# Up projection once per row pair with the signs joined on VectorE, and the down projection with stationary weights, in a float32 Fourier-mixing MLP

## The chip, the cores and the metric

The kernel runs on one core of a Trainium2 chip. The metric is the device time of one execution in microseconds (us), the median of three runs. Engines go by their short names: PE is TensorE (PEld its weight loads), DVE is VectorE, ACT is ScalarE, POOL is GpSimd, SP is SyncE, which here only issues DMAs. An engine works through its own instructions in order; it waits for another engine or for a DMA through semaphores.

## The reference

```python
X = np.fft.fft(x, axis=1); X = np.fft.fft(X, axis=2)     # x: (8, 3008, 256) float32
x = X.real.astype(np.float32).reshape(24064, 256)
h = x @ w_in                                             # (256, 2048)
g = np.maximum(0.01 * h, h)
return (g @ w_out).astype(np.float32)                    # (2048, 256)
```

Sequence and features of eight batches are mixed by a Fourier transform of which the real part is kept; a two-layer perceptron with a leaky ReLU follows. The weights arrive as float64.

## The kernel before

All arithmetic is float32. One `nc.tensor.matmul` of float32 operands is two PE instructions, each with a weight load of its own, so every count of the trace is twice that of the code.

The real part is cosine times cosine minus sine times sine. The rows of a batch are folded (row s with row S-s) by `fold_x`, so that the sequence transform needs only a quarter of the lengths, and the feature transform is multiplied into `w_in` once, on the chip (`w_in_part`), into the table `wf`. What is left per batch is `dft`: for a unit, that is a batch b and a half c of 377 or 376 frequencies, four products of six matmuls each give the even and odd parts of the cosine half (`mix0`) and of the sine half (`mix1`), and `butterfly` adds and subtracts them. A unit has a plus part and a minus part (`sg`), and each of these stands for two output rows that differ only in the sign of the sine half: a row pair.

A tile (list `tiles`) is one of these rows sets, 375 to 377 tokens; there are 4 in a unit, 64 in all. For each tile `up` goes over the 16 blocks of 128 hidden features: two matmuls into one PSUM bank, the cosine half with `wf[:, 0]` and the sine half with one of the two signed copies `wf[:, 1]` and `wf[:, 2]`; then ACT makes 0.01 times the bank (line 314) and DVE the maximum (line 315). `down` takes 128 tokens at a time as the stationary operand, streams the 256 columns of `w_out` past them, sums 16 blocks in one bank, and ACT copies it out (line 326) to be stored by SP, tokens in rows.

PSUM has eight banks: three for `up`, three for `dft`, two for `down`. The frequency d = 128 has no sine; it is computed for all batches in the start (`nyquist`) and a small DMA puts it into row 0 of `mix1`.

Two buffers, `xa` and `xb`, hold x of one batch: `xa` the rows, `xb` their mirrors, gathered by indirect DMAs that POOL issues. The folded rows end in `xb`. The next batch's rows may land when `dft` of the second half has read `xb` for the last time. In the start, eight pieces of `w_in` and then eight of `w_out` are loaded by SP and rounded from float64 to float32 by seven DVE instructions each (lines 214 to 220), through six buffers `g`.

A scheduler orders the instructions of each engine by its own estimate of time, so an engine's order differs from the order in the code.

Of the kernel before, what the change touches and what calls it, by code (L numbers as in the profile page):

```python
# [80 lines left out]
def feat_tables():  # L81
    """[j, (cosines 0..127 | cosine 128, -sines | cosine 128, +sines)], by shape alone."""
# [5 lines left out]
    out = np.zeros((D, 3, P), np.float32)  # L88
    out[:, 0] = cos
    for w, sign in ((1, -1.0), (2, 1.0)):  # L90
        out[:, w] = sign * sin
        out[:, w, 0:1] = nyq
    return out.reshape(D, 3 * P)
# [3 lines left out]
def tile_fnet_leaky_relu(  # L97
# [14 lines left out]
    work = ctx.enter_context(tc.tile_pool(name="work", bufs=1))  # L112
    ps = ctx.enter_context(tc.tile_pool(name="ps", bufs=1, space=PS))

    def up_ps():
        return ps.tile([P, 512], F32, tag="up", bufs=3, name="up_ps")

    def dft_ps():
        return ps.tile([P, 512], F32, tag="dft", bufs=3, name="dft_ps")
# [261 lines left out]
```

## Time and profile before

| | |
|---|---|
| time, median of 3 runs | 2948.84 us (2948.0 to 2951.03) |
| span of the profiled execution | 2950.5 us |
| PE busy | 2910.1 us, 99% |
| DVE busy | 707.3 us, 24% |
| ACT busy | 593.5 us, 20% |
| `down` on PE (line 323) | 45% of the chain that ended last |
| `up` on PE (line 311) | 44% |
| `dft` on PE (line 252) | 9% |

The chain that ended last is followed back from the last instruction, at each step to what released it. Here nearly all of it is PE, one instruction after another. The mean time of a matmul (479 ns) is longer than its distance from the next one, since matmuls are pipelined; distances are taken from runs of many matmuls in the chain.

### The profile page before, as it was taken

Reading aid. Unit: us, or ns where it says so; the run is one execution under the profiler, and the core shown is the slowest. Engines: PE = TensorE matmul, PEld = TensorE weight load, DVE = VectorE, ACT = ScalarE, POOL = GpSimd, SP = SyncE. Lnnn points to the kernel's source line nnn. Section 1 sums busy time; section 2 is a strip of 40 time slices with the busy share of each in tenths; the row PEclk is TensorE's granted clock in tenths of the full one; section 3 lists DMA queues with packets and bytes.
Section 4 is the critical chain, followed back from the end, with each engine's and each line's share of the span. In section 5 each row is a group of like instructions: output and inputs, shape, how many; then the busy total and the mean of one; then the engine's idle time right before and its main releaser. Section 6 shows DMA issues by size and latency. Waiting matters only on the chain.

```text
span 2950.5 us, 26768 instructions
## 1 busy us (share of the span) xinstructions
PE 2910.1 (99%) x11104; PEld 2090.8 (71%) x11104; DVE 707.3 (24%) x1270; ACT 593.5 (20%) x1279; POOL 79.1 (3%) x115
## 2 busy tenths in 40 slices
PE   4999999999999999999999999999999999999999
PEld 1667777777777677677677777777777776776777
DVE  6431221321222211221212212222212212112111
ACT  1121121221221211221221212212212112112211
POOL 2010000100001000000000000010000000000000
PEclk8999999999999999999999999999999999999999
DMA  8010000100001000010000000010000100000000
GB/s 295 18 50 11 7 9 11 50 9 9 9 9 51 7 11 11 9 50 9 7 11 27 32 11 7 9 51 9 9 11 6 32 11 6 11 10 7 11 11 11
DMA packets 40736, 69.24 MB, mean 23 GB/s; under 512 B 5942, under 2 KB 30374, under 8 KB 39590
## 3 DMA queue, kind: packets, MB, share of 16 engines
q1 hardware_dynamic: 31334, 33.53, 3.5%
q0 software_dynamic: 8128, 24.73, 2.7%
q10 hardware_dynamic: 1152, 9.27, 0.8%
q8 instruction: 87, 1.43, 0.2%
q14 instruction: 35, 0.29, 0.0%
HBM read 42.82 MB, written 24.64 MB: 23 GB/s over the span
## 4 chain that ended last, share of the span: by engine, by line
PE 98%; DMA 1%; DVE 1%; issue 0%; SPq 0%; ACT 0%; DVEq 0%
PE down_ps L323 45%; PE up_ps L311 44%; PE dft_ps L252 9%; DMA g<-in_w_in_dram 1%; DMA nya<-in_x_nyq_dram 1%; PE up_ps L234 0%; DVE xa L162 0%; DVE g L219 0%; DVE g L215 0%; DVE xb L170 0%; DVE xb L169 0%; DVE g L216 0%; DVE g L218 0%; DVE g L217 0%; DVE win L220 0%; DVE g L214 0%
## 5 line engine op out<-in xcount | busy, mean ns | idle before, releaser
L323 PE MATMUL down_ps<-wo,g 128*128 128x256 f32 x6144 | 1336.5, 379 | 0.0
L311 PE MATMUL up_ps<-mix,wf 128*128 128x376 f32 (+2 forms) x4096 | 1309.2, 479 | 0.0
L323 PEld LDWEIGHTS down_ps<-wo,g 128*128 128x128 f32 x6144 | 1153.3, 188 | 185.1
L311 PEld LDWEIGHTS up_ps<-mix,wf 128*128 128x128 f32 x4096 | 776.6, 190 | 505.3 <-issue 0.6
L315 DVE TENSOR_TENSOR g<-up_ps,leak 128x376 f32<-128x376 f32 (+2 forms) x1024 | 562.9, 550 | 1955.1 <-ACT leak L314 1955.1
L314 ACT ACTIVATE leak<-up_ps 128x376 f32<-128x376 f32 (+2 forms) x1024 | 495.4, 484 | 923.9 <-PE up_ps L311 920.8
L326 ACT COPY o<-down_ps 128x256 f32<-128x256 f32 (+2 forms) x192 | 71.4, 372 | 1185.8 <-PE down_ps L323 1185.8
L252 PE MATMUL dft_ps<-tab,xb 128*128 128x377 f32 (+3 forms) x768 | 248.5, 479 | 0.0
L252 PEld LDWEIGHTS dft_ps<-tab,xb 128*128 128x128 f32 (+1 forms) x768 | 145.4, 189 | 98.3 <-issue 0.6
L234 PE MATMUL up_ps<-win,feat_sb 128*128 128x512 f32 x48 | 30.9, 798 | 37.1 <-DVE win L220 18.7
L258 DVE TENSOR_TENSOR mix<-ev,dft_ps 128x377 f32<-128x377 f32 (+1 forms) x32 | 17.5, 547 | 198.4 <-PE dft_ps L252 198.4
L135 POOL DMA_DIRECT2D xb<-in_x_dram x8 | 4.0, 500 | 2158.0 <-PE dft_ps L252 2028.8
L234 PEld LDWEIGHTS up_ps<-win,feat_sb 128*128 128x128 f32 x48 | 11.4, 252 | 55.7 <-issue 29.0
L140 POOL DMA_INDIRECT xb<-in_x_dram,mirror x48 | 46.6, 971 | 21.7 <-issue 13.4
L257 ACT COPY ev<-dft_ps 128x377 f32<-128x377 f32 (+3 forms) x34 | 16.1, 472 | 124.0 <-PE dft_ps L252 124.0
L162 DVE TENSOR_TENSOR xa<-xa,xb 128x2550 f32<-128x2550 f32 (+1 forms) x16 | 28.0, 1748 | 31.8 <-DMA xb<-in_x_dram,mirror 31.8
L259 DVE TENSOR_TENSOR mix<-ev,dft_ps 128x377 f32<-128x377 f32 (+1 forms) x32 | 17.3, 541 | 0.0
L252 PE MATMUL dft_ps<-tab,nya 128*8 128x377 f32 (+3 forms) x48 | 15.7, 479 | 0.0
L171 ACT COPY xb<-xa 128x10 f32<-128x10 f32 (+1 forms) x16 | 3.2, 202 | 61.7 <-POOL xb L172 56.7
L170 DVE TENSOR_TENSOR xb<-xa 128x1270 f32<-128x1270 f32 (+1 forms) x16 | 15.1, 946 | 0.0
L169 DVE TENSOR_TENSOR xb<-xa 128x1270 f32<-128x1270 f32 (+1 forms) x16 | 15.1, 946 | 0.0
L235 ACT COPY wf<-up_ps 128x512 f32<-128x512 f32 x12 | 6.9, 585 | 39.5 <-PE up_ps L234 39.5
(25 smaller groups left out, 99.3 us busy)
## 6 DMA issues: line engine op xcount, KB each, us to landing
out_dram<-o SPq DMA_DIRECT2D x128, 128.0 KB
xa<-in_x_dram POOLq DMA_DIRECT2D x8, 1280.0 KB
tab<-in_seq_tab_dram ACTq DMA_DIRECT2D x8, 1131.0 KB
g<-in_w_in_dram SPq DMA_DIRECT2D x8, 512.0 KB
g<-in_w_out_dram SPq DMA_DIRECT2D x8, 512.0 KB
out_dram<-o SPq DMA_DIRECT2D x32, 120.0 KB
out_dram<-o SPq DMA_DIRECT2D x16, 121.0 KB
out_dram<-o SPq DMA_DIRECT2D x16, 119.0 KB
```

What stands on the lines that cost most here:

```text
L140: nc.gpsimd.indirect_dma_start(out=bv[0:n, i, :], out_offset=None, in_=pairs, in_offset=bass.IndirectOffsetOnAxis(ap=mirror[0:n, b, i : i ...
L162: nc.vector.tensor_tensor(a[:, :, :, 1:D], a[:, :, :, 1:D], m[:, :, ::-1, D - 1 : 0 : -1], op=ALU.add)
L234: nc.tensor.matmul(pt, lhsT=feat_sb[:, a, w * P : (w + 1) * P], rhs=win[a], start=(a == 0), stop=(a == 1))
L252: nc.tensor.matmul(ps_t[0:m, 0 : KW[c]], lhsT=z_of(i), rhs=tabs[n, c][0 : NV[i], i, 0 : KW[c]], start=(i == 0), stop=(i == NI - 1))
L257: nc.scalar.copy(ev[0:m, 0:kw], even_ps[0:m, 0:kw])
L258: nc.vector.tensor_tensor(plus, ev[0:m, 0:kw], odd_ps[0:m, 0:kw], op=ALU.add)
L259: nc.vector.tensor_tensor(minus, ev[0:m, 0:kw], odd_ps[0:m, 0:kw], op=ALU.subtract)
L311: nc.tensor.matmul(pt[:, 0:n], lhsT=wf[:, 0 if blk == 0 else w, fs], rhs=t[:, ::-1] if back else t, start=(blk == 0), stop=(blk == 1))
L314: nc.scalar.activation(leak[:, 0:n], pt[:, 0:n], ACT.Copy, bias=0.0, scale=SLOPE)
L315: nc.vector.tensor_tensor(g[:, f, 0:n], pt[:, 0:n], leak[:, 0:n], op=ALU.max)
L323: nc.tensor.matmul(pt[0:nr, 0:D], lhsT=hidden[j, f // FQ][:, f % FQ, t0 : t0 + nr], rhs=wo[:, f, :], start=(f == 0), stop=(f == NF - 1))
L326: nc.scalar.copy(o[0:nr, :], pt[0:nr, 0:D])
```

## The change

`tiles` goes; a block `(b, c, sg)` is a row pair, 32 in all. For one of its 16 hidden blocks (a step) `up` does the cosine half and the sine half once, each into a bank of its own. DVE then adds the d = 128 term, spread over all partitions (`nb`, one number `wn` per hidden feature), to the cosine bank, and forms the sum and the difference with the sine bank; ACT applies its leaky ReLU to both at once, in place. `down` takes `w_out` as the stationary operand and the hidden tokens as the moving one: two halves of the 256 output columns by two rows of the pair, summed over 16 steps in four banks. The result is stored transposed, [column, token], and the host puts it in order. `down` of a step follows `up` by two steps. `up` and `dft` share four banks.

Beside that, x and its mirrors come laid out by the host, so that two plain DMAs on SP load a batch into one buffer `xt`; the third copy in `wf` goes; the numbers `wn` take 32 matmuls of one column; the buffers for weights are three instead of six.

```diff
-        return ps.tile([P, 512], F32, tag="up", bufs=3, name="up_ps")
+    def up_ps(name="up_ps"):
+        return ps.tile([P, 512], F32, tag="up", bufs=4, name=name)
 ...
+        t = xp.tile([P, 2, NI, 2, D], F32, tag="x", bufs=1, name="xt")
+        for h in range(2):
+            nc.sync.dma_start(t[:, h], x[b, h])
 ...
+        nc.vector.tensor_tensor(s, s, z, op=ALU.add)
+        lo, hi = s[:, :, 1:P], s[:, :, P + 1 : D]
+        nc.vector.tensor_tensor(z[:, :, 1:P], lo, hi, op=ALU.add)
+        nc.vector.tensor_tensor(z[:, :, P + 1 : D], lo, hi, op=ALU.subtract)
 ...
-        return work.tile([P, FQ, KC], F32, tag="g", bufs=6, name="g").rearrange("p f k -> p (f k)")
+        return work.tile([P, 4, KC], F32, tag="raw", bufs=3, name="raw").rearrange("p f k -> p (f k)")
 ...
-        for w in range(3):
+        for w in range(2):
 ...
+        for i in range(WN // P):
+            for a in range(2):
+                nc.tensor.matmul(pt[:, i : i + 1], lhsT=win[a][:, i * P : (i + 1) * P],
+                                 rhs=feat_sb[:, a, 2 * P : 2 * P + 1], start=(a == 0), stop=(a == 1))
+        nc.scalar.copy(wn[:, f0 // P : f0 // P + WN // P], pt[:, 0 : WN // P])
 ...
+    def spread(u):
+        b, c = u
+        t = work.tile([P, 2, KC], F32, tag="nb", bufs=2, name="nb")
+        nc.sync.dma_start(t[:, :, 0 : KW[c]], nyq_dram[b, c, :, 0 : KW[c]].partition_broadcast(P))
+        spreads[u] = t
 ...
+    def up(j, f):
+        b, c, sg, _, n = blocks[j]
+        fs = slice(f * P, (f + 1) * P)
+        pt = [up_ps("cos_ps"), up_ps("sin_ps")]
+        for blk in range(2):
+            nc.tensor.matmul(pt[blk][:, 0:n], lhsT=wf[:, blk, fs], rhs=mixed[b, c][blk][:, sg, 0:n], start=True, stop=True)
+        cos = work.tile([P, KC], F32, tag="cos", bufs=3, name="cos")
+        nc.vector.scalar_tensor_tensor(cos[:, 0:n], in0=spreads[b, c][:, sg, 0:n], scalar=wn[:, f : f + 1],
+                                       in1=pt[0][:, 0:n], op0=ALU.mult, op1=ALU.add)
+        g = work.tile([P, 2, KC], F32, tag="g", bufs=5, name="g")
+        nc.vector.tensor_tensor(g[:, 0, 0:n], cos[:, 0:n], pt[1][:, 0:n], op=ALU.add)
+        nc.vector.tensor_tensor(g[:, 1, 0:n], cos[:, 0:n], pt[1][:, 0:n], op=ALU.subtract)
+        nc.scalar.activation(g[:, :, 0:n], g[:, :, 0:n], ACT.Lrelu)
+        hidden[j, f] = g
+
+    def down(j, f):
+        _, _, _, first, n = blocks[j]
+        if f == 0:
+            sums[j] = [[ps.tile([P, 512], F32, tag="sum", bufs=4, name="sum_ps") for _ in range(2)] for _ in range(2)]
+        g = hidden.pop((j, f))
+        for h in range(2):
+            for i in range(2):
+                nc.tensor.matmul(sums[j][h][i][:, 0:n], lhsT=wo[:, f, h * P : (h + 1) * P], rhs=g[:, i, 0:n],
                                  start=(f == 0), stop=(f == NF - 1))
 ...
+    lag = 2
+    for at in range(len(steps) + lag):
+        if at < len(steps):
+            j, f = steps[at]
+            up(j, f)
 ...
+            if sg == 1 and f == 10 and c == 0 and b + 1 < B:
+                load_x(b + 1)
+            if n + 1 < len(units):
+                if sg == 0 and f == 8:
+                    spread(units[n + 1])
+                    if c == 1:
+                        fold_x(b + 1)
+                if sg == 1 and f in (2, 8):
+                    dft(units[n + 1], f // 8)
+        if at >= lag:
+            down(*steps[at - lag])
```

How the instructions of an engine stand, at three places. First PE, in the middle of a unit of the first batch, before: the end of `up` of one tile and the beginning of `down` of the tile ahead of it (`wf` and `wo` are the weights, `g` the hidden tokens; the number behind a name is the buffer's).

```order
L311 MATMUL up_ps_547<-mix0_276,wf_84 128x376 [waits DVE_49]
L311 MATMUL up_ps_547<-mix1_295,wf_84 128x376
L311 MATMUL up_ps_553<-mix0_276,wf_84 128x376 [waits DVE_49]
L311 MATMUL up_ps_553<-mix1_295,wf_84 128x376
L311 MATMUL up_ps_559<-mix0_276,wf_84 128x376 [waits DVE_49]
L311 MATMUL up_ps_559<-mix1_295,wf_84 128x376
L323 MATMUL down_ps_565<-wo_85,g_421 128x256 x4
L323 MATMUL down_ps_565<-wo_85,g_446 128x256 x4
```

After, one and a half steps in the middle of a block; `wf` meets the cosine half `mix0` and the sine half `mix1` in banks of their own, and `wo` meets one `g` in four banks.

```order
L312 MATMUL cos_ps_530<-mix0_274,wf_74 128x377 [waits DVE_49]
L312 MATMUL sin_ps_531<-mix1_293,wf_74 128x377 [waits DVE_49]
L329 MATMUL sum_ps_452<-g_508,wo_76 128x377 [waits Activation_49]
L329 MATMUL sum_ps_453<-g_508,wo_76 128x377
L329 MATMUL sum_ps_454<-g_508,wo_76 128x377
L329 MATMUL sum_ps_455<-g_508,wo_76 128x377
L312 MATMUL cos_ps_546<-mix0_274,wf_74 128x377 [waits DVE_49]
L312 MATMUL sin_ps_547<-mix1_293,wf_74 128x377 [waits DVE_49]
```

Each hidden block of `up` was one bank with two matmuls; it is two banks with one each, and `down`, which was 48 matmuls of 256 columns in one stretch with a group of 16 for each bank, now comes in groups of four of 377 columns that visit four banks. Where there were four tiles in a unit, there are two blocks.

Second DVE, where x of the second batch is folded, before: `mix` is the second half of the unit's sine part, made when `dft` has ended, and lines 162 to 170 are `fold_x`.

```order
L258 TENSOR_TENSOR mix_700<-ev,dft_ps 128x376 [waits PE_49,Activation_49]
L259 TENSOR_TENSOR mix_700<-ev,dft_ps 128x376
L315 TENSOR_TENSOR g<-up_ps,leak 128x377 [waits Activation_49] x4
L162 TENSOR_TENSOR xa<-xa,xb 128x10x255 [waits DMASW6_49,DMASW2_49,DMASW7_49,DMASW1_49,DMASW0_49]
L163 TENSOR_TENSOR xa<-xa,xb 128x10
L162 TENSOR_TENSOR xa<-xa,xb 113x2x255 [waits DMASW5_49,DMASW4_49,DMASW3_49]
L163 TENSOR_TENSOR xa<-xa,xb 113x2
L169 TENSOR_TENSOR xb<-xa 128x10x127 [waits DVE_49,Pool_49]
L170 TENSOR_TENSOR xb<-xa 128x10x127
```

After, the same place; `xt` is the buffer of x, line 314 the new step on the cosine bank, lines 317 and 318 the sum and the difference.

```order
L269 TENSOR_TENSOR mix1_797<-ev_812,dft_ps_799 128x376
L314 SCALAR_TENSOR_TENSOR cos_824<-nb_312,wn_75,cos_ps_820 128x377 [waits PE_49]
L317 TENSOR_TENSOR g_826<-cos_824,sin_ps_821 128x377 [waits DVE_49,PE_49]
L318 TENSOR_TENSOR g_826<-cos_824,sin_ps_821 128x377
L314 SCALAR_TENSOR_TENSOR cos_838<-nb_312,wn_75,cos_ps_834 128x377 [waits PE_49]
L317 TENSOR_TENSOR g_840<-cos_838,sin_ps_835 128x377 [waits DVE_49,PE_49]
L318 TENSOR_TENSOR g_840<-cos_838,sin_ps_835 128x377
L314 SCALAR_TENSOR_TENSOR cos_855<-nb_312,wn_75,cos_ps_851 128x377 [waits PE_49]
L170 TENSOR_TENSOR xt_844<-xt_844 128x3072 [waits DMAHW3_49,DMAHW2_49,Pool_49]
L317 TENSOR_TENSOR g_857<-cos_855,sin_ps_852 128x377 [waits DVE_49,PE_49]
L318 TENSOR_TENSOR g_857<-cos_855,sin_ps_852 128x377
L314 SCALAR_TENSOR_TENSOR cos_869<-nb_312,wn_75,cos_ps_865 128x377 [waits PE_49]
L172 TENSOR_TENSOR xt_844<-xt_844 128x12x127 [waits DVE_49]
```

The fold is three large instructions instead of eight, and it stands between the instructions of the third, fourth and fifth steps behind the butterfly, though the code calls it later; the first of them waits for both halves of the load.

Third SP, at the beginning of the program, before:

```order
L177 DMA feat_sb_69<-in_feat_tab_dram 128x2x384
L198 DMA g_108<-in_w_in_dram 128x1024
L132 DMA nya_86<-in_x_nyq_dram 128x5x16
L133 DMA nya_86<-in_x_nyq_dram 112x16
L134 DMA nya_86<-in_x_nyq_dram 1x16
L135 DMA nyb_87<-in_x_nyq_dram 1x8
L198 DMA g_119<-in_w_in_dram 128x1024 [waits DMAHW0_49]
L136 DMA nyb_87<-in_x_nyq_dram 1x8 [waits DMAHW1_49]
L198 DMA g_142<-in_w_in_dram 128x1024 [waits DMAHW3_49]
L198 DMA g_153<-in_w_in_dram 128x1024 [waits DMAHW5_49,DMAHW2_49,DVE_49]
```

After:

```order
L180 DMA feat_sb_69<-in_feat_tab_dram 128x2x258
L160 DMA xt_71<-in_x_dram 128x3072 x2
L202 DMA raw_91<-in_w_in_dram 128x1024
L257 DMA nyx_77<-in_x_nyq_dram 128x192 [waits DMAHW0_49]
L202 DMA raw_102<-in_w_in_dram 128x1024 [waits DMAHW2_49]
L202 DMA raw_131<-in_w_in_dram 128x1024 [waits DMAHW4_49,DVE_49]
L202 DMA raw_142<-in_w_in_dram 128x1024 [waits DMAHW6_49,DVE_49]
L202 DMA raw_171<-in_w_in_dram 128x1024 [waits DMAHW2_49,DMAHW0_49,DVE_49]
```

The two loads of x, 1.5 MB each, which were issued by POOL on its own queue, now stand ahead of the first piece of `w_in` on SP's, and the third piece already waits for DVE, where before it was the fourth.

## Rows read from the trace of the kernel before

**Rows 1.** The page's part 1: busy time, share of the span and instructions.
```profile
...
PE 2910.1 (99%) x11104; PEld 2090.8 (71%) x11104; DVE 707.3 (24%) x1270; ACT 593.5 (20%) x1279; POOL 79.1 (3%) x115
...
```

**Rows 2.** Stretches: length, busy us (instructions) of each engine, granted clock, DMA share, GB/s.
```profile
...
0.00:98.90 98.90, 61.84 (x145) 24.48 (x145) 64.04 (x128) 10.38 (x19) 18.32 (x27) 0.90 0.66 231
98.90:2947.20 2848.30, 2848.29 (x10961) 2066.30 (x10960) 643.22 (x1142) 582.75 (x1259) 60.80 (x88) 1.00 0.05 16
2947.20:2950.50 3.30, 0.00 (x0) 0.00 (x0) 0.00 (x0) 0.37 (x1) 0.00 (x0) 1.00 0.14 37
...
```

**Rows 3.** Groups by line: operation, shapes, count, busy us, mean ns, idle before.
```profile
...
L323 PE MATMUL down_ps<-wo,g 128*128 128x256 f32 x6144 | 1336.5, 379 | 0.0
L311 PE MATMUL up_ps<-mix,wf 128*128 128x376 f32 (+2 forms) x4096 | 1309.2, 479 | 0.0
...
L315 DVE TENSOR_TENSOR g<-up_ps,leak 128x376 f32<-128x376 f32 (+2 forms) x1024 | 562.9, 550 | 1955.1 <-ACT leak L314 1955.1
L314 ACT ACTIVATE leak<-up_ps 128x376 f32<-128x376 f32 (+2 forms) x1024 | 495.4, 484 | 923.9 <-PE up_ps L311 920.8 <-DVE g L315 3.1
...
L234 PEld LDWEIGHTS up_ps<-win,feat_sb 128*128 128x128 f32 x48 | 11.4, 252 | 55.7 <-issue 29.0 <-DVE g L219 18.4 <-DVE win L220 8.3
...
L235 ACT COPY wf<-up_ps 128x512 f32<-128x512 f32 x12 | 6.9, 585 | 39.5 <-PE up_ps L234 39.5
...
```

**Rows 4.** Chain that ended last, 55 to 200 us: start, length, what.
```profile
...
60.36 8.37 PE up_ps L234 x12
68.73 30.20 PE dft_ps L252 x94
...
132.04 20.72 PE down_ps L323 x96
152.76 15.16 PE up_ps L311 x48
167.93 7.59 PE dft_ps L252 x24
...
```

**Rows 5.** Timeline, weight loads and conversions: start, length, instruction, idle time before it.
```profile
...
1.26 0.45 SPq L198 DMA_DIRECT2D g<-in_w_in_dram  x1
...
6.84 0.36 SPq L198 DMA_DIRECT2D g<-in_w_in_dram  x1
...
14.70 0.43 DVE L214 TENSOR_SCALAR g<-g 128x512 int32<-128x512 int32 x1 [14.70 <-DMA g<-in_w_in_dram]
...
21.36 0.43 DVE L214 TENSOR_SCALAR g<-g 128x512 int32<-128x512 int32 x1 [3.05 <-DMA g<-in_w_in_dram]
...
...
60.13 0.42 DVE L214 TENSOR_SCALAR g<-g 128x512 int32<-128x512 int32 x1
60.47 0.68 DVE L220 SCALAR_TENSOR_TENSOR win<-g 128x512 f32<-128x512 f32 x1
...
63.66 0.42 DVE L214 TENSOR_SCALAR g<-g 128x512 int32<-128x512 int32 x1
...
```

**Rows 6.** Timeline, reload and fold of x around 176 to 194 us.
```profile
...
176.06 0.50 POOL L135 DMA_DIRECT2D xb<-in_x_dram  x1 [129.15 <-issue]
...
183.69 0.93 POOL L140 DMA_INDIRECT xb<-in_x_dram,mirror  x1 [0.30 <-issue]
186.28 2.81 DVE L162 TENSOR_TENSOR xa<-xa,xb 128x2550 f32<-128x2550 f32 x1 [4.59 <-DMA xb<-in_x_dram,mirror]
...
193.88 0.94 POOL L132 DMA_DIRECT2D xa<-in_x_dram  x1 [3.93 <-DVE xb L170]
...
```

**Rows 7.** Stretches, transfer of the direct half of x.
```profile
...
195.00:200.00 5.00, 5.00 (x25) 4.24 (x24) 0.00 (x0) 0.00 (x0) 0.89 (x2) 1.00 0.89 264
200.00:205.00 5.00, 5.00 (x20) 3.29 (x19) 1.09 (x2) 1.35 (x3) 0.00 (x0) 1.00 0.30 95
...
```

**Rows 8.** Stretch in the start in which PE works with gaps.
```profile
...
20.00:30.00 10.00, 7.11 (x11) 2.36 (x9) 4.38 (x10) 1.67 (x3) 6.02 (x6) 0.83 1.01 368
...
```

**Rows 9.** Timeline, ACT at the end of the span.
```profile
...
2947.23 0.37 ACT L326 COPY o<-down_ps 120x256 f32<-120x256 f32 x1 [6.53 <-PE down_ps L323]
```

More of the change, by code (lines that the diff above doesn't have):

```diff
@@ L87, in feat_tables, with chunks, columns @@
     nyq = np.where(j % 2 == 0, 1.0, -1.0)
[L88 to L93, printed above, removed]
+    out = np.zeros((D, 2 * P + 2), np.float32)
+    out[:, 0:P] = cos
+    out[:, P : 2 * P] = -sin
+    out[:, 2 * P :] = nyq
+    return out
+def chunks():
+    out, at = [], 0
+    for b in range(B):
+        for c in range(2):
+            for sg in range(2):
+                out.append((b, c, sg, at, KW[c]))
+                at += 2 * KW[c]
+    return out, at
+def columns():
+    at = np.zeros(B * S, np.int64)
+    for b, c, sg, first, n in chunks()[0]:
+        k = K0[c] + np.arange(n)
+        plus, minus = (k, (S - k) % S) if sg == 0 else ((H + k) % S, H - k)
+        at[b * S + minus] = first + n + np.arange(n)
+        at[b * S + plus] = first + np.arange(n)
+    return at
 @with_exitstack
@@ L300, in tile_fnet_leaky_relu @@
-    hidden = {}
-    def up(j, fq):
-        u, sg, w, k, n, _, back = tiles[j]
-        g = work.tile([P, FQ, KC], F32, tag="g", bufs=6, name="g")
-        hidden[j, fq] = g
-        for f in range(FQ):
-            pt = up_ps()
-            fs = slice((fq * FQ + f) * P, (fq * FQ + f + 1) * P)
-            for blk in range(2):
-                t = mixed[u][blk][:, sg, k : k + n]
-                nc.tensor.matmul(pt[:, 0:n], lhsT=wf[:, 0 if blk == 0 else w, fs],
-                                 rhs=t[:, ::-1] if back else t, start=(blk == 0), stop=(blk == 1))
-            leak = work.tile([P, KC], F32, tag="leak", bufs=3, name="leak")
-            nc.scalar.activation(leak[:, 0:n], pt[:, 0:n], ACT.Copy, bias=0.0, scale=SLOPE)
-            nc.vector.tensor_tensor(g[:, f, 0:n], pt[:, 0:n], leak[:, 0:n], op=ALU.max)
@@ L317, in down @@
-    def down(j):
-        _, _, _, _, n, first, _ = tiles[j]
-        for t0 in range(0, n, P):
-            nr = min(P, n - t0)
-            pt = down_ps()
-            for f in range(NF):
-                nc.tensor.matmul(pt[0:nr, 0:D], lhsT=hidden[j, f // FQ][:, f % FQ, t0 : t0 + nr], rhs=wo[:, f, :],
-                                 start=(f == 0), stop=(f == NF - 1))
-            o = work.tile([P, D], F32, tag="o", bufs=4, name="o")
-            nc.scalar.copy(o[0:nr, :], pt[0:nr, 0:D])
-            nc.sync.dma_start(out[first + t0 : first + t0 + nr, :], o[0:nr, :])
+            sequence(pt, B, lambda i: nya[:, i, r, :], r, c)
@@ new lines, in tile_fnet_leaky_relu @@
+    units = [(b, c) for b in range(B) for c in range(2)]
+    blocks, _ = chunks()
+    steps = [(j, f) for j in range(len(blocks)) for f in range(NF)]
+    def up(j, f):
[12 more added lines that the diff above has]
+        hidden[j, f] = g
@@ new lines, in down @@
+    def down(j, f):
[6 more added lines that the diff above has]
+                nc.tensor.matmul(sums[j][h][i][:, 0:n], lhsT=wo[:, f, h * P : (h + 1) * P], rhs=g[:, i, 0:n],
+                                 start=(f == 0), stop=(f == NF - 1))
+        if f == NF - 1:
+            for h in range(2):
+                o = work.tile([P, 2, KC], F32, tag="o", bufs=2, name="o")
+                for i in range(2):
+                    nc.scalar.copy(o[:, i, 0:n], sums[j][h][i][:, 0:n])
+                nc.sync.dma_start(out[h * P : (h + 1) * P, first : first + 2 * n].rearrange("p (i n) -> p i n", i=2),
+                                  o[:, :, 0:n])
@@ L331, in tile_fnet_leaky_relu @@
     dft(units[0], 1)
+    spread(units[0])
     for n in range(4):
@@ L336, in tile_fnet_leaky_relu @@
     nyquist(1)
-    up(0, 0)
-    for j in range(len(tiles)):
-        n, at = divmod(j, 4)
-        b, c = units[n]
-        for fq in range(1, NF // FQ):
-            up(j, fq)
-        if at < 2 and n + 1 < len(units):
-            dft(units[n + 1], at)
-        if at == 1 and c == 0 and b + 1 < B:
-            load_x(b + 1)
-        if at == 3 and c == 0 and b + 1 < B:
-            fold_x(b + 1)
-        if j + 1 < len(tiles):
-            up(j + 1, 0)
-        down(j)
+    lag = 2
[3 more added lines that the diff above has]
+            up(j, f)
+            n, sg = divmod(j, 2)
+            b, c = units[n]
+            if sg == 1 and f == 10 and c == 0 and b + 1 < B:
[9 more added lines that the diff above has]
+            down(*steps[at - lag])
 def kernel(x, moe_w_in, moe_w_out):
```

106 lines of the change are left out of this document (34 added, 72 removed).

## The prediction

> **What bounds the kernel now.** I read the busy times first: PE is busy in 99% of the span, DVE in 24%, ACT in 20% [rows 1]. A share is an average, so I cut the span where the main loop begins, at its first `up` matmul, and at its last matmul [rows 2]: a start of 98.9 us, in which PE is busy for 61.8; a middle of 2848.3 us, in which it is busy for all of it at a granted clock of 1.00; a tail of 3.3 us. The chain of waits gives the price of an instruction, since the distance counts and not the mean duration of the groups (479 and 379 ns in [rows 3], which overlap): 48 of `up` in 15.16 us are 315.8 ns at 376 columns, 24 of `dft` in 7.59 are 316.3, 96 of `down` in 20.72 are 215.8 at 256 columns [rows 4]. Both are about 0.84 ns a column. The middle is their sum: 4096 of `up` at 315.8 make 1293.6, 6144 of `down` make 1326.1 [counts in rows 3], and `dft` of the 15 units after the first (720) 227.7; together 2847.4 of 2848.3. Nothing but the number of columns on PE sets the middle, and about 1 us in it is not explained by columns.
>
> **The change, part by part.**
>
> *The middle on PE.* A block has 16 steps; the 32 blocks have 512. A step is two `up` and four `down` matmuls in the code, twelve instructions, each over 377 or 376 columns. The nearest row is the `up` or `dft` instruction itself: 316.25 ns at 376.5 columns. So `up` falls from 4096 to 2048 instructions, 647.7 us (645.9 less); `down` goes from 6144 of 256 columns to 4096 of 376.5, 1295.4 (30.7 less, the 120-row remainders that streamed 256 columns like full ones). `dft` stays, 227.7; its last chunk now has 128 rows instead of 113, which adds no column. Sum 2170.8, with the unexplained 1 us 2171.8.
>
> *What has to lie beside it on DVE and ACT.* A step is 12 x 0.316 = 3.80 us of PE. DVE has three operations in it. One that reads a bank and another operand over 376 columns took 0.55 us [rows 3]; the kind with a scalar took 0.68 over 512 [rows 5], so at most 0.68 here. That is 1.65, at most 2.04 us a step. ACT has one operation over 754 elements in a row. Its rows are 484 ns for 376 and 585 for 512 [rows 3], 0.74 ns an element: about 0.77, and at most twice 484. Both fit into 3.80.
>
> *The waits.* From the end of a step's sine matmul to its own `down` PE has two groups of `down` and two of `up` to do, 2 x 2.53 + 2 x 1.27 = 7.6 us. In this time sum, difference and leaky ReLU must pass: 0.55 + 0.55 + 0.8 and two or three handovers, some 2.2 us. PE would come back to a bank of this step for the `up` two steps on after 6.3 us, when DVE needs 1.2. So 5 us of cover are left on both. Behind a `down` that waited would stand the next `up`, and DVE would wait for that. At the change of block the four sums must be copied: the first is complete three matmuls before the group ends, and PE has one `up` (1.27) before it writes there again; a copy is under 0.5 us, and the copies run one after another as fast as PE needs the banks. I count nothing for any of this, and up to 0.5 us a block, 16 in all, as the upper end.
>
> *The reload of x.* It may begin when `dft` of the second half ends, and DVE reaches the fold in the third step after that, about 11.4 us later (three groups of `down`, two of `up`, the cosine matmul of the third and its operation: 7.6 + 2.5 + 0.6 + 0.6). Now 3.1 MB must land in this time on SP's queue. Before, the gather of 1.5 MB began at 176.06, was issued until 184.6, and released the fold at 186.28, for which DVE stood 4.6 us [rows 6]; this cost PE nothing. The direct half of 1.5 MB was issued at 193.88 and moved at 264 GB/s at a DMA share of 0.89 [rows 6, 7]. By these 3.1 MB take 8.5 us (at the 368 of [rows 8]) to 12 (at 264), with the issue and landing some 10.5 to 14. When DVE waits for it, the third step's sum and difference wait behind the fold, and its sine bank with them; PE needs that bank 6.9 us after DVE came there. Of these the fold's first operation takes 2.81 x 3072/2550 = 3.4 [rows 6] and the two additions 1.1, so 2.4 us of lateness are covered. The load may thus take 11.4 + 2.4, about 14 us. I take nothing; the upper end is 20 us, which is 6 x 7 reloads = 42 us.
>
> *The start.* Before, the last folding of weights ended at 68.73, and 94 instructions of `dft` led to the first `up` in 30.2 [rows 4]. These 30 stay but for six that move ahead (2 us). What comes before them changes in three ways. The third folded copy goes, 16 instructions of 512 columns; 64 instructions of one column come, which no row shows; their weight loads are the nearest row, 252 ns on average in this stretch [rows 3], so 16 us, at four places, against at most 0.85 x 16 = 13.6 gained. Second, the loads of x are ahead of the first weights on SP, so DVE begins at about 20 to 25 us instead of 14.7 [rows 5], but it folds x then and not in the middle of the conversions. Third, three buffers instead of six let only two loads run ahead. A conversion takes 3.53 us (60.13 to 63.66), and the first two loads took 13.4 and 14.5 us beside tables and x [rows 5]. From below: x and weights as early as 14.7, the fold 7, eight conversions 28, the last matmuls 4, then 30: 84 us. From above: each pair of conversions waits for a load of 14.5, four pairs of 18 and the rest end at 121. Between: the second pair can only write its result when PE has read the first, so a pair costs some 6 us of PE and 4.2 of DVE after it; three of these after 32, the last 6, then 28 give 97. I take 98, near the 98.9 of before, and keep 84 and 121.
>
> *The tail.* The last copy is 0.1 us longer than the 0.37 of [rows 9], and the last store has 385 KB instead of 120; at 264 GB/s that is 1 us more. 3.3 becomes 4.4, between 3.3 and 6.
>
> *Sum.* 98 + 2171.8 + 4.4 = 2274 as a profiled span, 676 less than the 2950.5. The median of the runs is 1.7 us under the profiled span, so I say 2272.
>
> **A rule against it.** Before, PE walked through the three banks of `up` with a wait at nearly every one, and the clock stayed at 1.00 over the whole middle [rows 2]; in the start, with PE busy for 7.1 of 10 us, it was 0.83 [rows 8]. So the clock falls here when PE has gaps, and not because banks alternate. The Trainium skill, "TensorE: Matmul & The Clock Gate", section "A second HAM failure mode: psum-queue depth-cycling", tells of a kernel that cycles through PSUM banks, idles for moments between its groups of matmuls, and so falls back to half clock again and again. This kernel will change bank at every matmul. By that rule the next-to-last rival below would come; by the rows of before nothing would.
>
> **The rivals.**
>
> *The reload stalls PE.* For it: DVE did stand 4.6 us for x before, and twice the bytes now come in one go. Against it: they no longer pass POOL's ten instructions of issue. At 16 to 20 us for the load it costs 14 to 42 us: 2286 to 2314.
>
> *DVE or ACT becomes the bound of a step.* DVE goes from one operation in 1.26 us of `up` to three in 3.80. It needs 1.27 us for each of them before it decides, more than twice the row. At 1.5 us the 512 steps take 2304 instead of 1943, and the time is 2633. Against it is the row of 1024 operations at 0.55.
>
> *PE loses its clock.* If PE stops at the bank of every matmul, the level may fall from 2.4 to 1.2 GHz. Throughout, that doubles the 2171 us: 4443. It ends slower than before from the point at which 676 of the 2171, 31% of the work, run at the lower level. For it speaks the 0.83 of the start; against it the 5 us of cover and the middle at 1.00.
>
> *The change does not do what it says.* If PE did not shed the matmuls, it would stay at 2950. The order of its instructions has 1024 `up` and 2048 `down` in place of 2048 and 3072.
>
> **How the numbers follow.** The forecast, PE alone bounding the middle and a start like before, gets 0.86, with a range of its own from 2256 (start at 84) to 2300 (start at 121, and a few us of copies). The reload gets 0.07, DVE or ACT 0.03, the clock 0.03 (0.02 of it slower than before), no shedding 0.01. The range is 2255 to 2312, which leaves out the two rivals of a whole step and the worst reloads. A difference under 0.2%, about 6 us, could not be told from none. Faster 0.97, within 0.01, slower 0.02.
>
> **What would show it.** Right: PE busy in over 98% after the first 100 us at clock 1.00; the `up` and `down` instructions at a distance of 316 ns; DVE near 900 to 1000 us busy, ACT near 480 to 500, both idle mostly for PE; the fold waiting for x by no more than 2 us without a gap on PE behind it. Wrong: gaps of PE before `down` that end with ACT, or before a sine matmul that end with DVE, once a batch (reload) or once a step (DVE, ACT); a granted clock under 1.00 in the middle; a first `up` after 110 us. The forecast falls if the distance of matmuls in the middle is not 316.

## The result, and the profile after

| | before | after |
|---|---|---|
| time, median of 4 runs | 2949.82 us (2948.0 to 2951.03) | 2272.7 us (2272.32 to 2273.85) |
| span of the profiled execution | 2950.5 us | 2272.1 us |
| PE busy | 2910.1 us, 99% | 2229.8 us, 98% |
| DVE busy | 707.3 us, 24% | 963.7 us, 42% |
| ACT busy | 593.5 us, 20% | 502.7 us, 22% |

The ratio is 0.7705, with a 95% interval of 0.7694 to 0.7716: 677 us, 23%, are gone. The prediction said 2272.

Part 1 of the page of the changed kernel answers to [rows 1].

```profile
PE 2229.8 (98%) x7056; PEld 1329.0 (58%) x7056; DVE 963.7 (42%) x1741; ACT 502.7 (22%) x696; POOL 1.2 (0%) x12
```

PE has 4048 instructions fewer. DVE's busy time rose by over a third and that of ACT fell, and POOL, which gathered x before, is nearly gone.

The same cut into start, middle and tail as in [rows 2], with the same columns:

```profile
0.00:97.00 97.00, 58.85 (x196) 29.41 (x197) 66.22 (x125) 10.00 (x19) 0.32 (x5) 0.96 0.60 223
97.00:2267.60 2170.60, 2170.60 (x6861) 1299.61 (x6859) 897.45 (x1617) 491.95 (x676) 0.84 (x7) 1.00 0.07 24
2267.60:2272.10 4.50, 0.39 (x2) 0.00 (x0) 0.00 (x0) 0.74 (x2) 0.00 (x0) 1.00 0.46 171
```

In the middle PE is busy for the whole 2170.60 us at a granted clock of 1.00: what was true before is true after, with fewer columns. The chain of waits, in order of time (start, length, what), gives the price of a step, as in [rows 4]:

```profile
65.33 1.46 PE up_ps L243 x14
66.79 28.92 PE dft_ps L262 x90
95.71 0.83 PE cos_ps L312 x2
...
99.71 2.54 PE sum_ps L329 x8
...
103.51 2.54 PE sum_ps L329 x8
```

From one `down` group to the next, 99.71 to 103.51, it is 3.80 us for twelve instructions, 317 ns each. `up` begins at 95.71, where it began at 98.93 before.

The groups by line, which answer to [rows 3]:

```profile
L329 PEld LDWEIGHTS sum_ps<-g,wo 128*128 128x128 f32 x4096 | 777.1, 190 | 519.4 <-ACT g L319 0.2
L319 ACT ACTIVATE g<-g 128x752 f32<-128x752 f32 (+1 forms) x512 | 426.0, 832 | 1516.6 <-DVE g L318 1513.6
L314 DVE SCALAR_TENSOR_TENSOR cos<-nb,wn,cos_ps 128x376 f32<-128x376 f32 (+1 forms) x512 | 310.5, 607 | 1007.9 <-PE cos_ps L312 1007.9
...
L317 DVE TENSOR_TENSOR g<-cos,sin_ps 128x376 f32<-128x376 f32 (+1 forms) x512 | 280.3, 547 | 62.9 <-DVE cos L314 1.9
L318 DVE TENSOR_TENSOR g<-cos,sin_ps 128x376 f32<-128x376 f32 (+1 forms) x512 | 276.8, 541 | 0.0
```

The last column says who makes whom wait. Ahead of its operation on the cosine bank (line 314) DVE idles for 1007.9 us, all of it until PE has made that bank; ahead of the leaky ReLU ACT idles until DVE is done. In the other direction there is next to nothing: in the whole span the weight loads of `down` wait 0.2 us for ACT.

The reload of x, on SP and DVE, answers to [rows 6]. The timeline's rows are start, length, instruction; a number in brackets would be idle time of the engine before it:

```profile
209.39 0.61 DVE L314 SCALAR_TENSOR_TENSOR cos<-nb,wn,cos_ps 128x377 f32<-128x377 f32 x1 [2.09 <-PE cos_ps L312]
209.91 3.35 DVE L170 TENSOR_TENSOR xt<-xt 128x3072 f32<-128x3072 f32 x1
```

The load was issued at 198.64. The fold (line 170) starts as soon as the operation ahead of it is through: x had landed. The issues (shape and count, KB each, median us from issue to landing) say when, from 198 to 199 us, where the first half alone was issued, and in the whole stretch:

```profile
xt<-in_x_dram SPq DMA_DIRECT2D x1, 1536.0 KB, 6.1
```

```profile
xt<-in_x_dram SPq DMA_DIRECT2D x2, 1536.0 KB, 7.8
```

The 7.8 us are the median of the two halves, so the second one took 9.5. It was issued some 0.4 us after the first, and landed about 9.8 us after the first issue, about 1.5 us before DVE came to the fold; at the other six changes of batch 0.8 to 1.5 us were left. In the whole span DVE waits for x once, in the start (us in all, times, longest):

```profile
DVE xt L170 <- DMA xt<-in_x_dram: 22.3, 1, 22.3
```

### The profile page after: what moved, and what is told of

Its sections match the earlier page's. It is cut to its first block, busy times and chain, and to the rows that moved or that the text cites. A ratio compares the mean times of both kernels' runs of the same rounds, so it can differ in the third digit from the quotient of the medians.

```text
span 2272.1 us, 18025 instructions
## 1 busy us (share of the span) xinstructions
PE 2229.8 (98%) x7056; PEld 1329.0 (58%) x7056; DVE 963.7 (42%) x1741; ACT 502.7 (22%) x696; POOL 1.2 (0%) x12
## 4 chain that ended last, share of the span: by engine, by line
PE 98%; DMA 1%; DVE 1%; SPq 0%; issue 0%; ACT 0%; DVEq 0%
PE sum_ps L329 57%; PE cos_ps L312 14%; PE sin_ps L312 14%; PE dft_ps L262 11%; DMA raw<-in_w_in_dram 1%; PE up_ps L238 0%; PE up_ps L243 0%; DVE win L224 0%; DVE raw L223 0%; DVE raw L219 0%; DVE raw L222 0%; DVE xt L172 0%; DVE xt L173 0%; DVE raw L218 0%; DVE raw L221 0%; DVE raw L220 0%
## 5 line engine op out<-in xcount | busy, mean ns | idle before, releaser
L329 PE MATMUL sum_ps<-g,wo 128*128 128x377 f32 (+1 forms) x4096 | 1379.4, 479 | 0.0
L329 PEld LDWEIGHTS sum_ps<-g,wo 128*128 128x128 f32 x4096 | 777.1, 190 | 519.4 <-ACT g L319 0.2
L319 ACT ACTIVATE g<-g 128x752 f32<-128x752 f32 (+1 forms) x512 | 426.0, 832 | 1516.6 <-DVE g L318 1513.6
L314 DVE SCALAR_TENSOR_TENSOR cos<-nb,wn,cos_ps 128x376 f32<-128x376 f32 (+1 forms) x512 | 310.5, 607 | 1007.9 <-PE cos_ps L312 1007.9
L312 PE MATMUL sin_ps<-mix,wf 128*128 128x376 f32 (+1 forms) x1024 | 407.4, 479 | 0.0
L312 PE MATMUL cos_ps<-mix,wf 128*128 128x376 f32 (+1 forms) x1024 | 406.7, 478 | 0.0
L317 DVE TENSOR_TENSOR g<-cos,sin_ps 128x376 f32<-128x376 f32 (+1 forms) x512 | 280.3, 547 | 62.9 <-DVE cos L314 1.9
L318 DVE TENSOR_TENSOR g<-cos,sin_ps 128x376 f32<-128x376 f32 (+1 forms) x512 | 276.8, 541 | 0.0
L312 PEld LDWEIGHTS sin_ps<-mix,wf 128*128 128x128 f32 x1024 | 194.1, 190 | 129.9
L312 PEld LDWEIGHTS cos_ps<-mix,wf 128*128 128x128 f32 x1024 | 193.0, 189 | 130.9 <-issue 0.6
L262 PE MATMUL dft_ps<-tab,xt 128*128 128x377 f32 (+1 forms) x768 | 248.4, 479 | 0.0
```

The costliest lines, as they stand in the source:

```text
L262: nc.tensor.matmul(ps_t[0:m, 0 : KW[c]], lhsT=z_of(i), rhs=tabs[n, c][:, i, 0 : KW[c]], start=(i == 0), stop=(i == NI - 1))
L312: nc.tensor.matmul(pt[blk][:, 0:n], lhsT=wf[:, blk, fs], rhs=mixed[b, c][blk][:, sg, 0:n], start=True, stop=True)
L314: nc.vector.scalar_tensor_tensor(cos[:, 0:n], in0=spreads[b, c][:, sg, 0:n], scalar=wn[:, f : f + 1], in1=pt[0][:, 0:n], op0=ALU.mult, op1 ...
L317: nc.vector.tensor_tensor(g[:, 0, 0:n], cos[:, 0:n], pt[1][:, 0:n], op=ALU.add)
L318: nc.vector.tensor_tensor(g[:, 1, 0:n], cos[:, 0:n], pt[1][:, 0:n], op=ALU.subtract)
L319: nc.scalar.activation(g[:, :, 0:n], g[:, :, 0:n], ACT.Lrelu)
```

## The experiments

The theory after the result: PE's columns alone set the time, and the chain over DVE and ACT, the reload of x and the copies lie beside PE with room. The rivals ask how much room: whether DVE, the lag of `down`, or the reload is near a limit, and whether stops of PE would cost its clock.

**Halving undone, all else kept** (`e1_rows`). Each row of a pair gets its own two matmuls again, and DVE two operations instead of three; a third, negated copy of the sine half comes into `wf`:

```diff
 ...
-        for blk in range(2):
-            nc.tensor.matmul(pt[blk][:, 0:n], lhsT=wf[:, blk, fs], ...)
+        for row in range(2):
+            for blk in range(2):
+                nc.tensor.matmul(pt[row][:, 0:n], lhsT=wf[:, blk * (1 + row), fs], ...)
+            nc.vector.scalar_tensor_tensor(g[:, row, 0:n], in0=spreads[b, c][:, sg, 0:n], ...)
 ...
```

> Undoes the halving of the up projection alone: each row of a pair gets its own two matmuls again, with a third, negated table of the sine half, and everything else stays, the down projection with stationary w_out too. Theory (columns on PE set the time): 2048 more matmul instructions at 316 ns are 648 us, so 2272.7 + 648 = about 2920, within 8 us, and the rest to the 2949 of before, about 30 us, is what the down projection and the start gave. Rival (the gain came in good part from fewer waits and another order, not from columns): clearly less than 2900. Rival (PE had slack in a step): less than 2900 too.

Measured: 2920.61 us (2918.69 to 2922.39), ratio to before 0.9901 [0.9885, 0.9918]. The halving is worth 2920.61 - 2272.7 = 647.9 us, against the 647.7 of the sum (2048 instructions at 316.25 ns). What is left of the change, `down` transposed, the start and the rest, is worth 29 together; no run undoes one of them alone.

**One buffer `g` and a lag of one** (`e2_one_g`). The edit is `bufs=5` to `bufs=1` and `lag = 2` to `lag = 1`: the next sum cannot be written until `down` has read the last, so PE must stop for it.

> One buffer for the hidden tokens instead of five, and down one step behind up instead of two, so that sum and difference of a step can only be written when down of the step before has read them. PE then has a gap in each step. Theory: 2.53 us of down, then sum, difference and leaky ReLU 1.93 us and about 0.45 of handovers, 4.9 us a step instead of 3.8; at full clock about 2810 to 2830 us, granted clock 1.00, PE idle about 1.1 us a step. Rival (gaps at every bank take the clock away): granted clock well under 1.00 in the middle, at half clock 7.5 us a step and some 4300 us. Rival (handovers cost nothing): 4.5 us a step, 2600.

Measured: 2834.22 us in one run, a little above the expectation. A step on PE and DVE, PE's waits in the whole span (us in all, times, longest), and the middle (columns as in the cut above):

```profile
1003.12 0.90 PE L312 MATMUL sin_ps<-mix,wf 128*128 128x376 f32 x2 [1.17 <-DVE g L318]
...
1003.86 0.80 PE L312 MATMUL cos_ps<-mix,wf 128*128 128x376 f32 x2
1004.50 2.69 PE L329 MATMUL sum_ps<-g,wo 128*128 128x376 f32 x8
1007.29 0.55 DVE L317 TENSOR_TENSOR g<-cos,sin_ps 128x376 f32<-128x376 f32 x1 [3.59 <-PE sum_ps L329]
...
1008.36 0.90 PE L312 MATMUL sin_ps<-mix,wf 128*128 128x376 f32 x2 [1.17 <-DVE g L318]
```

```profile
PE sin_ps L312 <- DVE g L318: 432.7, 387, 1.5
```

```profile
97.00:2800.00 2703.00, 2271.17 (x6811) 1224.76 (x6810) 888.13 (x1605) 496.44 (x669) 0.83 (x7) 1.00 0.05 20
```

This step takes 5.24 us (1003.12 to 1008.36) instead of 3.80. PE stands 1.17 us in it, and 0.27 us more are lost where its matmuls no longer overlap: the `down` group takes 2.69 us to its end, where another group would have started after 2.53, and the first two behind the stop take 0.74 instead of 0.63. PE stops in this way in 387 of the 512 steps. So the total came near the expectation with a longer step, but in fewer steps than expected, which is partly luck. What bears on the rival is the clock: it stays at 1.00. The section that the prediction weighed (the Trainium skill, "TensorE: Matmul & The Clock Gate", "A second HAM failure mode: psum-queue depth-cycling") tells of a bf16 kernel that goes back and forth between half and full clock, because it cycles through banks and idles for moments. This trace does not agree: PE changes bank at every matmul and idles in three steps of four, at a granted clock of 1.00.

**More work on DVE** (`e3_three_more_on_dve`, `e4_six_more_on_dve`). Behind the operation on the cosine bank stand three or six more additions, whose result nothing uses:

```diff
+        for _ in range(3):
+            more = work.tile([P, KC], F32, tag="more", bufs=2, name="more")
+            nc.vector.tensor_tensor(more[:, 0:n], cos[:, 0:n], pt[1][:, 0:n], op=ALU.add)
```

> Three more additions on VectorE in each step, of the same operands as the sum, written to a buffer that nobody reads, ahead of the sum in its chain. VectorE then has six operations in a step of 3.8 us of PE. Theory (PE columns alone): 6 x 0.55 = 3.3 us still fit, and the chain to down gets 1.4 us longer, inside the 5 us of cover: 2273 to 2277, within noise. Rival (VectorE is close to the bound of a step, at the fold of x above all): 7 folds that cost some us each, 2290 or more.

> Six more such additions instead of three: nine operations on VectorE in a step. Theory, by the distance of queued operations in the trace after (0.46 us from one start to the next, 0.6 for the first): 4.2 to 4.3 us a step, VectorE becomes the bound, and the time is 2330 to 2370. Theory by the durations that the prediction used (0.55 each, 4.97 a step): about 2700 to 2750. Rival (VectorE does not bound at all): 2273.

Measured: with three 2273.03 us (2272.17 to 2274.95), ratio 0.7705 [0.7692, 0.7718], nothing lost; with six 2436.24 in one run, between the two numbers expected. Part 1 of the two pages, three first:

```profile
PE 2230.2 (98%) x7056; PEld 1329.0 (58%) x7056; DVE 1660.5 (73%) x3277; ACT 510.0 (22%) x696; POOL 1.1 (0%) x12
```

```profile
PE 2355.9 (97%) x7056; PEld 1290.7 (53%) x7056; DVE 2291.7 (94%) x4813; ACT 507.1 (21%) x696; POOL 1.2 (0%) x12
```

With six, the added operations of a step on DVE and the sum behind them:

```profile
1000.87 2.84 DVE L318 TENSOR_TENSOR more<-cos,sin_ps 128x377 f32<-128x377 f32 x6
1003.61 0.56 DVE L320 TENSOR_TENSOR g<-cos,sin_ps 128x377 f32<-128x377 f32 x1
```

An addition lasts 0.55 us, but six in a row end after 2.84: they start 0.46 apart. Nine operations are 9 x 0.46 = 4.1 us, over PE's 3.80. DVE decides from somewhere between six and nine operations a step; the change has three. The expectation by starts left out DVE's other work in the middle (folds and butterflies) and its waits: it still idles 83.4 us until PE has made a cosine bank.

**x loaded twice** (`e5_reload_twice`) **and a lag of one** (`e6_lag1`): in the first each half of x of a later batch comes twice in a row, in the second only `lag = 2` becomes `lag = 1`.

> The changed kernel, but at each of the seven changes of batch x is loaded a second time into the same tiles behind the first load, so that the fold waits for about twice as much transfer; the result is the same. Theory (the reload is hidden only because it ends before DVE is ready for the fold, and some 2.4 us more of delay at the fold would still lie in the cover of the up projection): the first load takes at most 11 us (issue at 198.6, fold at 209.9 without waiting), so the pair takes about 21 us, DVE waits some 10 us at the fold, 2.4 of them covered, and TensorE loses about 7.4 us seven times, 52 us: about 2325 us. Rival A (there is far more room, and the transfer is hidden anyway): 2273. Rival B (no cover at all, the whole wait reaches TensorE): about 2341.

> The changed kernel with the down projection of a unit one step behind its up projection instead of two. Theory (two steps of lag leave 7.6 us between the sine matmuls and the unit's own down matmuls, against a chain over DVE and ScalarE of about 2.4 us; one step leaves 3.8 us, which still covers an ordinary step, but not the fold's 3.35 us on DVE at a change of batch): ordinary steps cost nothing, each of seven changes of batch costs 2 to 2.6 us, in all 14 to 18 us: 2287 to 2291 us. Rival (the chain with its handovers is longer than 3.8 us, so every step waits): over 0.2 us in each of 512 steps, 2375 us or more. Rival (the second step of lag is not needed anywhere): 2273.

Measured: 2272.53 us (2270.97 to 2272.63), ratio 0.7703 [0.7691, 0.7714], and 2273.61 (2271.66 to 2277.47), ratio 0.7706 [0.7694, 0.7717]: neither costs anything. Both expectations missed, for one reason: the scheduler works the order out anew from its own estimates. DVE's fold with x loaded twice (issue at 197.33):

```profile
217.32 3.35 DVE L171 TENSOR_TENSOR xt<-xt 128x3072 f32<-128x3072 f32 x1
```

It comes 20.0 us after the issue instead of 11.3, over two steps later, and again waits for nothing, so this run does not test what a late load costs. With a lag of one, the chain at the fold:

```profile
218.10 0.63 PE cos_ps L312 x2
218.73 0.63 PE sin_ps L312 x2
219.37 0.63 PE cos_ps L312 x2
220.00 0.71 PE sin_ps L312 x2
220.71 0.63 PE cos_ps L312 x2
221.35 5.07 PE sum_ps L329 x16
```

Where `down` would have to wait for the fold, three further `up` matmuls are put ahead of it. In the other steps `down` follows one step behind, and 3.8 us cover the chain. So the second step of lag is not needed, with the order that the scheduler then takes: this rival stands.

**x late, with the fold held in its place** (`e8_pinned_two`, `e9_pinned_three`, control `e11_pinned_one`). The fold's first operation gets a call of its own, one step after `load_x`, and a one-column operation behind it rewrites, unchanged, a number that the next step reads, so no later step passes it:

```diff
         nc.vector.tensor_tensor(s, s, z, op=ALU.add)
+        if b:
+            nc.vector.scalar_tensor_tensor(wn[:, 12:13], in0=s[:, 0, 0:1], scalar=0.0,
+                                           in1=wn[:, 12:13], op0=ALU.mult, op1=ALU.add)
 ...
+            if sg == 1 and f == 11 and c == 0 and b + 1 < B:
+                fold_add(b + 1)
```

> As the run with x loaded twice, but the fold's place on DVE is held: its first operation is followed by one on a single column that rewrites (unchanged) the numbers wn which the next step's operation on the cosine bank reads, so that no later step can pass the fold. The result is the same. In the run before, the two pairs were on their way for 17.7 us after the issue, and DVE, as it stands here, is ready for the fold 12.4 us after the issue, so it must stand 5.3 us. Theory (work in flight covers some of it: the down matmuls of the next step are reached 10.3 us after DVE is ready, and DVE and ScalarE need 8.2 from the fold's start, so 2.1 us are covered): TensorE stops for 3.2 us seven times, 22 us: about 2296 us. Rival (no cover): 5.3 times 7, 37 us: 2310. Rival (a wait of DVE this long is hidden altogether): 2273.

> The same with three loads of each pair: on their way for 25.6 us, so DVE stands 13.2 us at the fold. Theory (2.1 us covered): 11.1 times 7, 78 us: about 2351 us. Rival (no cover): 2365. Rival (the wait is hidden): 2273. Between this and the run with two, each us of lateness must cost one us per change of batch if the cover is used up.

> The control of the two pinned runs: the fold's place on DVE is held in the same way, and x is loaded once. Theory (the hold itself costs nothing, 512 rows of a pair step are unchanged and one operation on one column comes seven times; the losses of the pinned runs are the late load's): 2273, and no idle time of TensorE before a cosine matmul. Rival (the hold, by moving 5 us of fold in front of the next step's operation, stalls TensorE on its own): some 3 to 6 us seven times, 2294 to 2315.

Measured: one load 2274.21 us (2271.04 to 2278.41), ratio 0.7712 [0.7699, 0.7725]; two 2312.67 (2307.15 to 2316.69), ratio 0.7838 [0.7825, 0.785]; three 2371.19 (2363.98 to 2374.53), ratio 0.8033 [0.8019, 0.8046]. Holding the fold costs nothing; against the control two loads cost 38 us and three 97, where 22 and 78 were expected. Waits in the whole span (engine and line, releaser: us in all, times, longest; the longest on x is that of the start), first with two, then with three loads:

```profile
DVE xt L170 <- DMA xt<-in_x_dram: 63.7, 8, 21.1
...
PE cos_ps L321 <- DVE cos L323: 19.9, 7, 3.4
```

```profile
DVE xt L170 <- DMA xt<-in_x_dram: 124.6, 8, 22.5
...
PE cos_ps L321 <- DVE cos L323: 79.5, 7, 13.4
```

Without the start DVE stood 42.6 / 7 = 6.1 and 102.1 / 7 = 14.6 us a batch, PE 2.8 and 11.4. So some 3.2 us are covered in both, 1.1 more than expected; PE's stops are near the 3.2 and 11.1 of the theory because DVE also stood longer than the 5.3 and 13.2 expected. But the time grew by more than PE stood. The middle, from the first cosine matmul to the last matmul, with one, two and three loads (columns as in the cut above):

```profile
95.29:2267.66 2172.37, 2172.35 (x6865) 1300.47 (x6864) 899.40 (x1626) 492.22 (x676) 0.84 (x7) 1.00 0.07 24
```

```profile
96.36:2307.95 2211.59, 2188.68 (x6865) 1305.68 (x6864) 899.88 (x1626) 492.09 (x676) 0.83 (x7) 0.99 0.09 34
```

```profile
98.56:2367.47 2268.91, 2189.43 (x6865) 1307.10 (x6864) 899.81 (x1626) 492.25 (x676) 0.84 (x7) 0.98 0.11 43
```

It grew by 39.2 and 96.5 us. PE was idle for 22.9 and 79.5 of them (with two loads, 3.0 of the 22.9 before `down`, for ACT), and was busy for 16.3 and 17.1 us longer with the same instructions: 2.3 and 2.4 us a batch. The chain with two loads shows where this lies, and the cut of the same stretch the clock:

```profile
224.04 1.63 PE cos_ps L321 x2
...
230.92 0.63 PE cos_ps L321 x2
```

```profile
220.70:224.00 3.30, 0.15 (x1) 0.00 (x0) 3.27 (x5) 0.21 (x1) 0.12 (x1) 0.84 0.00 0
224.00:227.50 3.50, 3.46 (x6) 1.94 (x7) 3.50 (x7) 1.67 (x2) 0.00 (x0) 0.50 0.00 0
```

After a stop of 3.2 us the granted clock is 0.50, the 1.2 GHz level, and the step behind it takes 6.88 us instead of 3.80. Not every stop had this price. At the fifth change of batch in the same run PE stands 2.38 and then 0.84 us, and the clock stays:

```profile
1337.00:1350.00 13.00, 9.78 (x31) 5.50 (x30) 10.30 (x17) 3.54 (x5) 0.12 (x1) 1.00 0.11 31
```

So a late load is paid twice: by the stop, and mostly also by a stretch of half clock behind it, 2.3 to 2.4 us a batch on average for the short stops and the long ones. From two loads to three DVE stands 8.5 us a batch longer and the middle grows by 8.2: beyond the cover a us of lateness costs about one.

**The start in another order** (`e7_start`, `e10_start_warm`). The first part of `w_in` comes ahead of x, `dft` of unit 0 ahead of the last parts of `w_in`, and most of `w_out` between the first steps; the second kernel also gives PE 64 matmuls of zeros in the 17 us in which it has nothing to do.

```diff
-    load_x(0)
 ...
-    for f0 in range(0, F, WN):
-        w_in_part(f0)
+    w_in_part(0)
+    load_x(0)
 ...
+    for f0 in range(WN, F, WN):
+        w_in_part(f0)
 ...
+        if at <= 10 and at % 2 == 0:
+            w_out_part(at + 4)
```

> The changed kernel with its start in another order: the first part of w_in ahead of x on the load queue, the DFT of unit 0 and the Nyquist column ahead of the remaining parts of w_in, and the parts of w_out transposed between the steps of the first block. Nothing is left out. Theory (the first 95.6 us before the first cosine matmul are set by TensorE's own instructions plus a wait for x of about 22 us; w_out's 13 to 16 us and part of the wait can be moved beside or into later work): the first cosine matmul comes 10 to 20 us earlier, but what is moved still costs TensorE its own columns, so that the time is 5 to 18 us less, about 2258 us. Rival (the loads of the weights set the start, whatever the order): 2270 to 2276. Rival (transposes between steps hold up the evictions of the first block): 2276 to 2290.

> The kernel with the start in another order, and 64 matmuls of 128 columns of zeros ahead of it, in the 17 us in which TensorE has nothing to do; nothing reads their bank. Theory (TensorE's first 20 us of real work ran at the lower of its two clock levels: 4 matmuls in 3.78 us and 14 of one column in 2.78, and 16 of the Nyquist column at 0.63 instead of 0.32, about 6.5 us too long, because it had stood still before): with work ahead of them they run at the higher level, and the time falls by up to 6.5 us: 2258. Rival (the 4.2 us in which TensorE then waits for the second half of w_in lower the clock again): 2263 to 2266, as without. Rival (the added matmuls run at the lower level throughout, 15.5 us or more, and hold up the first part): 2266 to 2272.

Measured: 2264.51 us (2259.37 to 2264.74), ratio 0.7672 [0.7661, 0.7682], which lies wholly below the 0.7694 to 0.7716 of the change: a gain of 8 us, at the lower end of what was expected. Its first cosine matmul comes at 74.17 instead of 95.64, more than 20 us earlier, but most of what was moved then stands between the steps. With the zeros it is 2262.03 (2261.55 to 2262.77), ratio 0.7669 [0.7659, 0.768], not told apart from the first and just under what its first rival said. So both beat the changed kernel, by 8 to 11 us. The stretch behind those 17 us, first as ordered, then with the zeros:

```profile
17.00:37.00 20.00, 15.65 (x34) 7.27 (x35) 14.48 (x22) 2.73 (x5) 0.12 (x1) 0.66 0.80 318
```

```profile
17.00:37.00 20.00, 12.63 (x48) 6.22 (x48) 12.20 (x16) 2.82 (x6) 0.12 (x1) 0.83 0.93 371
```

With the zeros the clock is 0.83 instead of 0.66, but PE then stands 7.4 us for the second piece of `w_in` instead of 4.2, which takes part of it back.

## Why the prediction was right

*The total.* 2272 were forecast and 2272.7 measured; that they are so close is in part luck. The span was forecast at 2274.2 and is 2272.1: the start was given 2.3 us too much, the tail 0.3 too much, the middle 0.5 too little. The 1.7 us taken off to come to the median were a misreading. Before, the profiled execution had a span longer than the median of the others; but each execution takes some 1.8 us more than its own span (2273.85 for 2272.1), and the median after lies 0.6 above the profiled span. The two errors nearly cancel.

*The middle.* 2171.8 us were forecast; from the first cosine matmul at 95.71 to the last matmul's end at 2267.99 it is 2172.3. The reason is shown: 647.9 against 647.7 for the halving, by undoing it; for the `down` that walks through four banks, which was not undone alone, by the distance of 317 ns in the chain.

*DVE and ACT.* The additions were priced at 0.55 us and took 0.547 and 0.541; the operation on the cosine bank took 0.61, inside its bounds; ACT took 0.83 instead of 0.77, and is busy for 502.7 us where 480 to 500 were named. None of it was on the path: three more operations cost nothing. That DVE decides from 1.27 us an operation was right as a statement on the step; in operations of this size there is room for at least three more.

*The waits.* The 5 us of cover were more than is needed: with one step of lag nothing is lost. No copy at a change of block cost anything that the chain shows.

*The reload.* It was priced at 10.5 to 14 us and taken as hidden. It was there about 9.8 us after its issue, and DVE came to the fold after 11.3, where 11.4 were counted, so the fold waited for nothing, with 0.8 to 1.5 us to spare. Of the rates the upper one, 368 GB/s [rows 8], was near, with about 1.5 us for issue and landing where 2 were added. The cover was 3.2 us where 2.4 were counted, so by an estimate from these numbers a load 4 us later would still have been hidden. What the rival left out is the clock: with a load late beyond the cover, the batch costs some 2.3 us more than PE stands.

*The start.* 98 us were forecast, 95.7 came. Two prices in it were too high, and they partly cancel. The 64 one-column matmuls were given 252 ns each, 16 us; the chain has 14 of them in 1.46, 104 ns each, or some 7 us in all. The 16 instructions of 512 columns that went were given up to 13.6 us; at full clock four take 1.95, so 16 are 7.8. In the sum, the foldings were to end at 32 + 3 x 10.2 + 6 = 68.6 and ended at 66.79, `dft` took 28.9 instead of 28, and 97 had been rounded to 98. In the same stretch the clock fell: four `w_in` instructions that take 1.95 us took 3.78.

```profile
47.29 1.62 PE L243 MATMUL up_ps<-feat_sb,win 128*128 128x1 f32 x14
49.56 2.67 PE L238 MATMUL up_ps<-win,feat_sb 128*128 128x512 f32 x4 [0.65 <-DVE win L224]
...
53.12 3.78 PE L238 MATMUL up_ps<-win,feat_sb 128*128 128x512 f32 x4 [0.66 <-DVE win L224]
...
59.35 1.95 PE L238 MATMUL up_ps<-win,feat_sb 128*128 128x512 f32 x4 [0.65 <-DVE win L224]
```

```profile
49.56:50.50 0.94, 0.94 (x3) 0.46 (x4) 0.94 (x3) 0.00 (x0) 0.00 (x0) 1.00 0.25 31
...
51.50:52.46 0.96, 0.95 (x3) 0.35 (x2) 0.82 (x3) 0.00 (x0) 0.00 (x0) 0.50 0.68 277
```

By 51.5 us the granted clock was 0.50, so it fell while the matmuls that began at 49.56 ran, before the stop of 0.66 us. Ahead of it lie 14 one-column matmuls and stops of 1.50 and 0.65 us; which of these let it fall was not tried.

*The clock as a rival.* It got 0.03. Changing bank at every matmul did not cost it: the middle is at 1.00, and it stays so with a stop of 1.17 us in most steps. Where it fell in the middle of other runs, PE had stopped once for longer: for 2.7 to 3.4 us in six of seven changes of batch with two loads, for over 10 us in all with three. No limit follows from this, since one stop of 2.38 us left it at 1.00, and in the run with six more additions a single stop of 1.76 us was followed by a `down` group of 4.49 us instead of 2.69:

```profile
280.62 0.90 PE L312 MATMUL sin_ps<-mix,wf 128*128 128x376 f32 x2 [1.76 <-DVE g L321]
281.57 4.49 PE L332 MATMUL sum_ps<-g,wo 128*128 128x376 f32 x8
```

The Trainium skill, "TensorE: Matmul & The Clock Gate", "HAM oscillation — how this bites in real kernels", describes waits after which the next group of matmuls starts cold and loses half of that stretch. The late loads agree in those six changes; in the one shown, 3.1 us are lost in a step of 6.88.

## What to carry to other kernels

Where PE is busy for the whole of a stretch at full clock, the time is its columns: count them, price them by the distance in the chain and not by the mean duration, and then only ask whether everything else fits beside them. A linear step that is done twice with one sign changed can be done once and joined on an idle engine, as long as that engine's starts, not its durations, fit into PE's step. An experiment on a kernel with a scheduler must hold the order, or it measures the scheduler's answer.

## What the runs showed beside that

- Operations of DVE that queue start closer together than they last: 0.46 us apart at 0.55 us each. A load judged by durations is too high by a fifth.
- A stop of PE costs more than it lasts. Stops of 1.17 us made a step 1.44 us longer, at clock 1.00, for the lost overlap of matmuls; at the late loads, stops of 2.8 us on average cost 5.6 a batch, and of 11.4 us 13.8, mostly with a stretch of half clock behind them.
- 3.1 MB of x in two plain loads were there about 9.8 us after the issue, where the gather of the mirrors alone, 1.5 MB, had taken some 10 before.
